# Top-8 from the gate columns, a TensorE transpose ahead of the down projection, and the down projection three half blocks earlier, in a fused state-space and routed-MLP kernel

## The chip, the cores and the metric

One core of a Trainium2 chip runs the whole kernel. The metric is the device time of one execution in microseconds (us), as the median of several runs. The profile is one further execution; its span is the time from its first to its last instruction.

## The reference

All large tensors are bf16. L is 2048 tokens, D is 1024 channels, P is 1024 states, and F is 3584.

```python
g = sigmoid((x * gate_w).sum(-1))                 # one gate for each token
# branch a: a diagonal complex state space layer
Bu = x @ B_bar.T                                  # complex, 1024 states
h_t = Lam_bar * h_{t-1} + Bu_t                    # scan over 2048 tokens
a = 2 * Re(hseq @ C.T) + x * Dskip
# branch b: an MLP on the 8 tokens with the largest score
r = x @ w_r ; idx = argsort(-r)[:8]
y = (silu(x[idx] @ w_gate) * (x[idx] @ w_up)) @ w_down * sigmoid(r[idx])
b = x ; b[idx] += y
out = g * a + (1 - g) * b
```

## The kernel before

**Stages.** The tokens are cut into 8 chunks k of 256. S1 multiplies x with the B matrices for a pair of chunks at a time (`s1`, PE line 266; `s1x`, line 282, for the first ones). ScalarE (ACT) copies the result from PSUM to V. VectorE (DVE) rotates it, scans it and rotates it back (`dve_m`, `dve_scan`, `dve_post`) into H[k]. S2 multiplies H[k] with the C matrices (`s2`, PE line 768): a chunk has two row blocks b of 128 tokens, and each row block has two halves dh of 512 channels, with 16 matmuls for a half. ACT then scales the half by the gate into ot (line 773). From block 2 on, ACT first presets the PSUM tile with x*D (`preset`, line 742, `KX = 1`); blocks 0 and 1 get x*(g*D + 1-g) by another way (`scale_x`, `mul_e`). The term (1-g)*x is written to the output by a DMA (`skip_x`), and `fin(b)` adds ot to it by an accumulating DMA on POOL's queue (line 794). The last two blocks add on DVE and are written by SyncE's queue (SP).

**The order.** It is written out by hand. PE, DVE, ACT and SP take their work exactly in program order. A list `blocks` gives the main loop, and its index n is the stage: n = 0 is S1 of chunks 2 and 3, n = 1 and 2 are S2 of chunks 0 and 1, n = 3 is S1 of chunks 4 and 5, n = 4 and 5 are S2 of chunks 2 and 3, n = 6 is S1 of chunks 6 and 7, and n = 7, 8, 9, 10 are S2 of chunks 4 to 7. `at((n, t), fn)` puts a piece of work into stage n: within an S2 stage, t below 1 means after the first half, t below 2 after the second, and so on.

**The router.** `gate_rows` (PE line 486) computes the scores r and the gate logits as rows: four groups of 512 tokens on partitions 0, 32, 64, 96. `gate_cols` turns them by four 128x128 TensorE transposes (zt, line 493) into columns, one column for each 128 tokens, and makes gcol and omgcol. The top 8 are found in two steps. `sel_a` copies the score rows (128 x 512) and `sel_a2` takes 8 candidates out of each row with DVE's max and index operations. `sel_b` gathers the 4 x 8 candidates of the four rows with one matmul (fl_ps, line 536), `sel_b2` takes the final 8 of 32 and starts the gather of their x rows (xsel). `sel_c` transposes xsel (xselT_ps, line 573).

**The MLP.** Its weights come in slots over SP's queue (`load_w`: wgu for gate and up, wd and wdb for down). `moe_slot` runs them on PE between the S2 and S1 stages: gate and up into pgu (line 660), later the down projection into y4 (the profile's y, line 672) as 112 matmuls that use 32 columns of the array each. Between the two, `silu_a` and `silu_b` make the gated activations gr1, and `silu_t` turns them into aT with a DMA transpose on SP's queue:

```python
def silu_t():
    nc.sync.dma_start_transpose(M["aT"][:].rearrange("p c j s -> p c (j s)"), M["gr", 1][:])
```

The last act is `sel_d` (the gate of the 8 tokens, zs_ps, line 589), `fin_a` (ACT copies y out as yc), `sel_c2`, `sel_d2` and `fin_b` (four small DVE operations on yc), `scatter_upd` (an accumulating indirect DMA on POOL's queue, line 752, then a read of the update ul for the last chunk on SP's), and `add_upd` on DVE for the last two blocks. The places of these in the list:

```python
at((7, 0.97), silu_t)
at((9, 2.88), sel_d)
at((9, 2.92), fin_a)
at((9, 2.95), lambda: (sel_c2(), sel_d2(), fin_b(), scatter_upd()))
pos = ... [(7, 0.9)] * 2 + [(9, 2.9)] * 7      # the 7 slots of the down projection
```

PSUM tiles of the router and the MLP share two buffers (pool `ps_m`, tag m), in turn; S2's tiles have two of their own.

Of the kernel before, what the change touches and what calls it, by code (L numbers as in the profile page):

```python
# [9 lines left out]
ALU = mybir.AluOpType  # L10
F32 = mybir.dt.float32
BF16 = mybir.dt.bfloat16
I32 = mybir.dt.int32
U32 = mybir.dt.uint32
PSUM = bass.MemoryType.PSUM

P = 128
LC = 256
# [6 lines left out]
def kernel(  # L25
# [19 lines left out]
    nc = tc.nc  # L45
# [6 lines left out]
    NTT = L // P  # L52
# [3 lines left out]
    NSEL = 8  # L56
# [9 lines left out]
    small = ctx.enter_context(tc.tile_pool(name="small", bufs=1))  # L66
    ps_s1 = ctx.enter_context(tc.tile_pool(name="ps_s1", bufs=2, space=PSUM))
    ps_s2 = ctx.enter_context(tc.tile_pool(name="ps_s2", bufs=2, space=PSUM))
    ps_m = ctx.enter_context(tc.tile_pool(name="ps_m", bufs=2, space=PSUM))
# [60 lines left out]
    ident = const.tile([P, P], BF16, name="ident")  # L130
    from concourse.masks import make_identity
    make_identity(nc, ident[:])
    ramp = const.tile([P, LC], F32, name="ramp")
    nc.gpsimd.iota(ramp[:], pattern=[[1, LC]], base=0, channel_multiplier=0, allow_small_or_imprecise_dtypes=True)
    jrow8 = small.tile([8, 4, 8], F32, name="jrow8")
    nc.gpsimd.iota(jrow8[:], pattern=[[2 * LC, 4], [0, 8]], base=LC, channel_multiplier=0, allow_small_or_imprecise_dtypes=True)
    M = {}
    rg = small.tile([P, KD, 32], BF16, name="rg")
    nc.gpsimd.memset(rg[:], 0.0)
    ones8 = small.tile([P, 8], BF16, name="ones8")  # L140
    nc.gpsimd.memset(ones8[:], 1.0)
    for i, v in enumerate((B_w_r, gate_w)):
        nc.gpsimd.dma_start(vrow[:, 3 + i, :], v.rearrange("(c p) -> c p", p=P))

# [329 lines left out]
    def sigm(pool, z_ap, shape, tagp):  # L474
        e = pool.tile(shape, BF16, name=tagp + "_e", tag={"sl": "mg"}.get(tagp, tagp))
        nc.scalar.activation(out=e[:], in_=z_ap, func=ACT.Sigmoid)
        return e

    gcol = small.tile([P, NTT], F32, name="gcol")
    omgcol = small.tile([P, NTT], F32, name="omgcol")  # L480

# [8 lines left out]
    def gate_cols():  # L490
        zt = ps_m.tile([P, 4, P], BF16, name="zt", tag="m")
        for tq in range(4):
            nc.tensor.transpose(zt[:, tq, :], M["zrb"][:, tq * P:(tq + 1) * P], ident[:])  # L493
        zv = zt[:].rearrange("p t (j s) -> p j t s", s=32)
        zb = small.tile([P, NTT], BF16, name="zb")
        nc.scalar.copy(out=zb[:].rearrange("p (j t) -> p j t", t=4), in_=zv[:, :, :, 1])
        gb = sigm(small, zb[:], [P, NTT], "gc")
        nc.scalar.copy(out=gcol[:], in_=gb[:])
        ob = small.tile([P, NTT], BF16, name="ob")
        nc.scalar.activation(out=ob[:], in_=gb[:], func=ACT.Copy, scale=-1.0, bias=1.0)  # L500
        nc.scalar.copy(out=omgcol[:], in_=ob[:])
        M["aT"] = small.tile([P, NFC // 4, 4, 32], BF16, name="aT", tag="va")

    nc.scalar.dma_start(Dbc[:], A_Dskip.rearrange("(o d) -> o d", o=1).to_broadcast([P, D]))
    M["xsel32"] = small.tile([P, KD, 32], BF16, name="xsel32", tag="wt")
# [2 lines left out]
    rowp = ctx.enter_context(tc.tile_pool(name="rowp", bufs=1))  # L508
# [3 lines left out]
    AX = mybir.AxisListType.X  # L512

    def sel_a():
        rT = rowp.tile([P, 2 * LC], F32, name="rT", tag="row8")
        nc.scalar.copy(out=rT[:], in_=M["zrb"][:])
        M["rT"] = rT

    def sel_a2():
        rT = M["rT"]  # L520
        mA = rowp.tile([P, NSEL], F32, name="mA")
        iA = rowp.tile([P, NSEL], U32, name="iA")
        nc.vector.max(out=mA[:], in_=rT[:])
        nc.vector.max_index(out=iA[:], in_max=mA[:], in_values=rT[:])
        iAf = rowp.tile([P, NSEL], F32, name="iAf")
        nc.vector.tensor_scalar(out=iAf[:], in0=iA[:], scalar1=-float(LC), scalar2=None, op0=ALU.add)
        mm = rowp.tile([P, 2, 4, NSEL], BF16, name="mm", tag="mg")
        eyeb = ident[:, 0:P:32].unsqueeze(2).to_broadcast([P, 4, NSEL])
        nc.vector.tensor_tensor(out=mm[:, 0], in0=mA[:].unsqueeze(1).to_broadcast([P, 4, NSEL]), in1=eyeb, op=ALU.mult)
        nc.vector.tensor_tensor(out=mm[:, 1], in0=iAf[:].unsqueeze(1).to_broadcast([P, 4, NSEL]), in1=eyeb, op=ALU.mult)  # L530
        M["mm"] = mm

    def sel_b():
        mm = M["mm"]
        fl_ps = ps_m.tile([NSEL, 2, 4 * NSEL], F32, name="fl_ps", tag="m")
        nc.tensor.matmul(fl_ps[:].rearrange("p k n -> p (k n)"), lhsT=ones8[:], rhs=mm[:].rearrange("p k j s -> p (k j s)"), start=True, stop=True)
        fl = rowp.tile([NSEL, 2, 4 * NSEL], F32, name="fl", tag="gr0")
        nc.scalar.copy(out=fl[:], in_=fl_ps[:])
        M["fl"] = fl

    def sel_b2():
        fl = M["fl"]
        cv = fl[:, 0, :]
        ci = rowp.tile([NSEL, 4 * NSEL], F32, name="ci", tag="mg")
        nc.vector.tensor_tensor(out=ci[:], in0=fl[:, 1, :], in1=jrow8[:].rearrange("p j s -> p (j s)"), op=ALU.add)
        gm = rowp.tile([NSEL, NSEL], F32, name="gm")
        kx = rowp.tile([NSEL, NSEL], U32, name="kx")
        nc.vector.max(out=gm[:], in_=cv)
        nc.vector.max_index(out=kx[:], in_max=gm[:], in_values=cv)
        kxf = rowp.tile([NSEL, NSEL], F32, name="kxf")  # L550
        nc.vector.tensor_copy(kxf[:], kx[:])
        dtmp = rowp.tile([NSEL, 2, NSEL], F32, name="dtmp")
        nc.vector.tensor_tensor(out=dtmp[:, 0, :], in0=kxf[:], in1=ident[:NSEL, :NSEL], op=ALU.mult)
        nc.vector.tensor_tensor(out=dtmp[:, 1, :], in0=gm[:], in1=ident[:NSEL, :NSEL], op=ALU.mult)
        dsel = rowp.tile([NSEL, 2], F32, name="dsel")
        nc.vector.reduce_sum(out=dsel[:], in_=dtmp[:], axis=AX)
        eq = rowp.tile([NSEL, 4 * NSEL], F32, name="eq", tag="gr1")
        nc.vector.tensor_scalar(out=eq[:], in0=ramp[:NSEL, 0:4 * NSEL], scalar1=dsel[:, 0:1], scalar2=None, op0=ALU.is_equal)
        nc.vector.tensor_tensor(out=eq[:], in0=eq[:], in1=ci[:], op=ALU.mult)
        tokf = rowp.tile([NSEL, 1], F32, name="tokf")  # L560
        nc.vector.reduce_sum(out=tokf[:], in_=eq[:], axis=AX)
        idx_c = small.tile([NSEL, 1], I32, name="idx_c")
        nc.vector.tensor_copy(idx_c[:], tokf[:])
        M["idx_c"] = idx_c
        xsel = rowp.tile([NSEL, D], BF16, name="xsel", tag="row8")
        nc.gpsimd.indirect_dma_start(out=xsel[:], out_offset=None, in_=x2d, in_offset=bass.IndirectOffsetOnAxis(ap=idx_c[:, :1], axis=0))
        M["xsel"] = xsel
        M["dsel"] = dsel
# [10 lines left out]
    def sel_c2():  # L579
        rs_b = M["rs_e"]  # L580
        rsel_c = small.tile([NSEL, 1], F32, name="rsel_c")
        nc.vector.tensor_copy(rsel_c[:], rs_b[:])
        M["rsel_c"] = rsel_c
# [10 lines left out]
    def sel_d2():  # L594
        gs_b = M["gs_e"]
        omg_b = rowp.tile([NSEL, 1], BF16, name="omg_b")
        nc.vector.tensor_scalar(out=omg_b[:], in0=gs_b[:], scalar1=-1.0, scalar2=1.0, op0=ALU.mult, op1=ALU.add)
        omg32 = small.tile([NSEL, 1], F32, name="omg32")
        nc.vector.tensor_copy(omg32[:], omg_b[:])
        M["omg32"] = omg32  # L600

    NG = 4
# [3 lines left out]
    NFB = FG // P  # L606
# [73 lines left out]
        nc.vector.tensor_tensor(out=up[:], in0=sl[:], in1=up[:], op=ALU.mult)  # L680

    def silu_t():
        nc.sync.dma_start_transpose(M["aT"][:].rearrange("p c j s -> p c (j s)"), M["gr", 1][:])

    def fin_a():
        yc = rowp.tile([NSEL, D], BF16, name="yc", tag="row8")
# [4 lines left out]
    def fin_b():  # L691
        yb = M["yc"]
        nc.vector.tensor_scalar(out=yb[:], in0=yb[:], scalar1=M["rsel_c"][:, 0:1], scalar2=M["omg32"][:, 0:1], op0=ALU.mult, op1=ALU.mult)
        M["upd"] = yb
# [56 lines left out]
    def scatter_upd():  # L751
        nc.gpsimd.indirect_dma_start(out=out2d[:, :], out_offset=bass.IndirectOffsetOnAxis(ap=M["idx_c"][:, :1], axis=0), in_=M["upd"][:], in_offset=None, bounds_check=L - 1, oob_is_err=False, compute_op=ALU.add)
        M["ul"] = const.tile([P, BPC, D], BF16, name="ul", tag=free_w.pop(0))
        nc.sync.dma_start(M["ul"][:], out2d[TLAST:, :].rearrange("(r p) d -> p r d", p=P))
# [48 lines left out]
    def at(pos, fn):  # L803
        pending.append((pos, len(pending), fn))
# [24 lines left out]
    at((2, 2.2), lambda: (scale_x(1), mul_e(1), load_x(5)))  # L829
    at((2, 3.5), lambda: (fin(0), fin(1)))  # L830
    at((3, 3.9), sel_c)
    at((9, 2.88), sel_d)
    at((3, 1.2), lambda: dve_m(3, 0, 8))
    at((3, 2.3), lambda: (skip_d(2), dve_scan(3, 0, 8)))
    at((3, 6.5), lambda: (skip_d(3), dve_post(3, 0, 8)))
# [21 lines left out]
    at((7, 0.96), silu_b)  # L857
    at((7, 1.2), lambda: (dve_scan0(6, 4, 8), dve_state(6, 0, 8)))
    at((7, 2.5), lambda: fin(8))
    at((7, 0.97), silu_t)  # L860
    at((7, 3.95), lambda: fin(9))
    at((7, 3.5), lambda: dve_post(6, 0, 8))
    at((7, 3.4), lambda: skip_d(6))
# [4 lines left out]
    at((9, 1.2), lambda: skip_x(14))  # L868
    at((9, 2.2), lambda: skip_x(15))
    at((8, 2.5), lambda: fin(10))  # L870
    at((9, 2.92), fin_a)
    at((8, 3.95), lambda: fin(11))
    at((9, 0.0), lambda: (skip_d(7), last_post(0, 0, NCT)))
    at((9, 0.1), lambda: last_m(1))
    at((9, 0.95), lambda: last_scan(1))
    at((9, 2.95), lambda: (sel_c2(), sel_d2(), fin_b(), scatter_upd()))
    at((9, 2.5), lambda: fin(12))
    at((9, 3.95), lambda: fin(13))
    at((9, 3.0), lambda: (last_post(1, 0, NCT // 2), last_post(1, NCT // 2, NCT)))
    at((10, 0.5), lambda: (add_upd(NTT - 2), add_upd(NTT - 1)))  # L880

    pos = [(3, 4.9)] * 2 + [(4, 1.9)] * 3 + [(5, 1.9)] * 3 + [(6, 1.9)] * 3 + [(6, 5.9)] * 3 + [(7, 0.9)] * 2 + [(9, 2.9)] * 7
    for s in range(NW // 2):
        at(pos[s], lambda s=s: moe_slot(s))

# [8 lines left out]
    for n, (m, k) in enumerate(blocks):  # L894
        free_w.extend(fill.get(n, ()))
        if n == 7:
            for pl in range(2):
                t = const.tile([P, 4, 2, D], BF16, name="wdb", tag=f"BT{pl}")
# [48 lines left out]
```

## Time and profile before

| | |
|---|---|
| median of 3 runs | 248.1 us (247.72 to 248.26) |
| profiled execution | 248.1 us, span 246.3 us |
| granted TensorE clock | 1.0 over the whole span |
| busy share | PE 98%, DVE 92%, ACT 48%, POOL 11% |
| instructions | 3573, of them PE 1405 matmuls and as many weight loads |
| DMA | 48.48 MB, 197 GB/s mean |

The 1.8 us between span and time lie outside the first and the last instruction. PE and DVE are both almost always busy, so the shares alone do not say which of them sets the time; the chain of waits does. A busy PE in these rows is a matmul's modelled start to end, and matmuls overlap, so costs on PE are read from the distance between groups and not from the busy time of one instruction.

### The profile page before, as it was taken

To read this page: it belongs to the slowest core of one execution; us is meant where nothing else is said; L and a number is where in the kernel's file an instruction comes from. 1 tells how busy PE (TensorE), PEld (TensorE's weight loads), DVE (VectorE), ACT (ScalarE), POOL (GpSimd) and SP (SyncE) were. 2 spreads that over 40 slices of the span, in tenths; PEclk is the share of its full clock that TensorE was granted. 3 is DMA by queue.
4 is the path that set the end of the run, shared out by engine and by line. 5 is a ranking of instruction groups with operands and counts; after the bars stand their busy time and mean duration, and the time that the engine had idled before them with its cause. 6 is when DMAs were issued, how large, how long until landed. Compare 5 with 4: busy or idle time off the path is not lost.

```text
span 246.3 us, 3573 instructions
## 1 busy us (share of the span) xinstructions
PE 240.7 (98%) x1405; PEld 115.3 (47%) x1405; DVE 225.8 (92%) x229; ACT 119.3 (48%) x203; POOL 26.9 (11%) x47
## 2 busy tenths in 40 slices
PE   8899999999999999999999999999999999999994
PEld 6664444444444444444444444444444444446453
DVE  1899999999999999999999999999999999999932
ACT  3699973233462572223355462235266445456411
POOL 4000000000000301520002040100000211110210
PEclk9999999999999999999999999999999999999999
DMA  7999999999760440766257989776699999962062
GB/s 187 224 135 244 226 229 217 276 215 257 253 191 0 118 140 0 150 108 213 88 190 229 352 230 320 239 285 249 184 359 284 385 304 302 111 128 35 3 146 69
DMA packets 65249, 48.48 MB, mean 197 GB/s; under 512 B 50496, under 2 KB 52160, under 8 KB 65232
## 3 DMA queue, kind: packets, MB, share of 16 engines
q1 hardware_dynamic: 60048, 37.46, 58.9%
q0 software_dynamic: 3264, 7.38, 14.5%
q10 hardware_dynamic: 1920, 3.41, 4.1%
q8 instruction: 11, 0.18, 0.3%
q14 instruction: 6, 0.05, 0.1%
HBM read 27.55 MB, written 8.40 MB: 146 GB/s over the span
## 4 chain that ended last, share of the span: by engine, by line
PE 95%; DMA 2%; SPq 1%; DVE 0%; issue 0%
PE vps L266 42%; PE zps L768 42%; PE zps L784 3%; PE pgu L660 3%; PE vps L282 2%; DMA BT<-in_A_B_im_dram 2%; PE y L672 1%; SPq L80 1%; PE zr L486 1%; SPq L77 0%; DVE ot L789 0%; PE xselT_ps L573 0%; PE zs_ps L589 0%; PE zt L493 0%; PE vb_ps L437 0%
## 5 line engine op out<-in xcount | busy, mean ns | idle before, releaser
L768 PE MATMUL zps<-CT,H 128*128 128x512 bf16 x480 | 105.0, 379 | 0.0
L266 PE MATMUL vps<-X,BT 128*128 128x512 bf16 x480 | 105.0, 379 | 0.0
L266 PEld LDWEIGHTS <-BT 128*128 128x128 bf16 x480 | 46.6, 98 | 56.8 <-PE pgu L660 0.7
L768 PEld LDWEIGHTS <-H 128*128 128x128 bf16 x480 | 46.5, 98 | 56.6 <-issue 1.3
L313 DVE TENSOR_TENSOR_SCAN U<-d,U 128x2048 bf16<-128x2048 f32 (+2 forms) x22 | 62.0, 2859 | 1.0 <-DVE U L304 0.5
L273 ACT CAST V<-vps 128x512 bf16<-128x512 f32 x60 | 32.2, 588 | 58.9 <-PE vps L266 58.8
L773 ACT ACTIVATE ot<-zps,gcol 128x512 bf16<-128x512 f32 x30 | 20.6, 686 | 46.3 <-PE zps L768 46.3
L742 ACT CAST zps<-xd 128x512 f32<-128x512 bf16 (+1 forms) x29 | 16.6, 576 | 3.6 <-ACT xt L729 3.3
L302 DVE TENSOR_TENSOR U<-V,T2tab 128x4096 bf16<-128x4096 bf16 (+2 forms) x11 | 16.6, 1511 | 0.6
L303 DVE TENSOR_TENSOR V<-V,nTi 128x4096 bf16<-128x4096 bf16 (+2 forms) x11 | 16.7, 1516 | 0.5
L304 DVE TENSOR_TENSOR U<-U,V 128x4096 bf16<-128x4096 bf16 (+2 forms) x11 | 16.7, 1516 | 0.4
L794 POOL DMA_DIRECT2D out_dram<-ot x14 | 13.0, 928 | 30.3 <-ACT ot L773 30.3
L338 DVE TENSOR_TENSOR U<-U,S2tab 128x4096 bf16<-128x4096 bf16 x7 | 16.0, 2292 | 0.2
L340 DVE TENSOR_TENSOR H<-H,U 128x4096 bf16<-128x4096 bf16 x7 | 16.0, 2292 | 0.2
L706 POOL DMA_DIRECT2D xt<-in_A_x_dram x12 | 7.2, 596 | 83.5 <-DMA out_dram<-xt 41.4
L729 ACT ACTIVATE xt<-xt,omgcol 128x1024 bf16<-128x1024 bf16 x14 | 16.0, 1144 | 0.0
L336 DVE TENSOR_TENSOR H<-U,Ctab 128x4096 bf16<-128x4096 bf16 x7 | 16.0, 2283 | 0.0
L371 DVE TENSOR_TENSOR_SCAN U<-D,U 128x1024 bf16<-128x1024 f32 x4 | 8.9, 2278 | 0.1
L724 DVE TENSOR_TENSOR xd<-xt,Dbc 128x1024 bf16<-128x1024 bf16 x14 | 9.0, 683 | 0.0
L282 PE MATMUL vps<-X,BT 128*128 128x256 bf16 x64 | 7.5, 273 | 1.2 <-DMA BT<-in_A_B_re_dram 0.6
L660 PE MATMUL pgu<-wgu,xsel 128*32 128x448 bf16 x128 | 7.2, 354 | 0.0
L282 PEld LDWEIGHTS <-BT 128*128 128x128 bf16 x64 | 6.0, 98 | 2.4 <-DMA BT<-in_A_B_re_dram 0.9
(155 smaller groups left out, 138.8 us busy)
## 6 DMA issues: line engine op xcount, KB each, us to landing
wgu<-in_B_w_gate_dram SPq DMA_DIRECT2D x16, 448.0 KB, 5.6
wgu<-in_B_w_up_dram SPq DMA_DIRECT2D x16, 448.0 KB, 6.6
out_dram<-ot POOLq DMA_DIRECT2D x14, 256.0 KB, 5.4
wdb<-in_B_w_down_dram SPq DMA_DIRECT2D x7, 512.0 KB, 10.5
xt<-in_A_x_dram POOLq DMA_DIRECT2D x12, 256.0 KB, 3.5
out_dram<-xt ACTq DMA_DIRECT2D x12, 256.0 KB, 5.4
wd<-in_B_w_down_dram SPq DMA_DIRECT2D x5, 512.0 KB, 10.3
xt<-in_A_x_dram SPq DMA_DIRECT2D x4, 256.0 KB, 4.2
```

The lines of the kernel that those rows point to most:

```text
L266: nc.tensor.matmul(o, lhsT=BT[pl][:, dc, ct * P:(ct + 1) * P], rhs=X[m][:, dc, k0 * LC:k1 * LC], start=(dc == 0), stop=(dc == KD - 1))
L273: nc.scalar.copy(out=V[k][:, :, ct, :], in_=vp[m, ct][:, :, kk, :])
L282: nc.tensor.matmul(vps[:, pl, c, :], lhsT=BT[pl][:, dc, ct * P:(ct + 1) * P], rhs=X[0][:, dc, k * LC:(k + 1) * LC], start=(dc == 0), stop= ...
L302: nc.vector.tensor_tensor(out=u, in0=v, in1=T2tab[:, :, c0:c1, :], op=ALU.mult)
L303: nc.vector.tensor_tensor(out=v, in0=v, in1=bc(nTi, c0, c1), op=ALU.mult)
L304: nc.vector.tensor_tensor(out=u, in0=u, in1=V[k][:, ::-1, c0:c1, :], op=ALU.add)
L313: nc.vector.tensor_tensor_scan(out=fl, data0=d0[:, c0:c1, :].rearrange("p c t -> p (c t)"), data1=fl, initial=0.0, op0=ALU.mult, op1=ALU.add)
L336: nc.vector.tensor_tensor(out=h, in0=g, in1=bc(Ctab, c0, c1), op=ALU.mult)
L338: nc.vector.tensor_tensor(out=g, in0=g, in1=S2tab[:, :, c0:c1, :], op=ALU.mult)
L742: nc.scalar.copy(out=z[:], in_=xd[b][:, d_:d_ + w])
L768: nc.tensor.matmul(zps[:], lhsT=H[k][:, pl, ct, tl * P:(tl + 1) * P], rhs=CT[pl][:, ct, dsl], start=(fresh and ct == 0 and pl == 0), stop= ...
L773: nc.scalar.activation(out=ots[b][:, dsl], in_=zps[:], func=ACT.Copy, scale=gcol[:, b:b + 1])
```

## The change

The note that comes with the change says that row blocks 2 and 3 also have x*D preset in PSUM, and that their (1-g)*x and the fp32 product of block 0 moved into S2 of chunks 0 and 1. The diff has no edit of `preset`, `KX`, `scale_x`, `skip_x` or of their places in the list: they are the same in both kernels. What the diff holds is this.

- The first step of the top 8 works on 16 rows of 128 tokens in place of 4 rows of 512. `gate_cols` keeps the score columns (rcb), `sel_a` transposes them on PE to 16 x 128 (rT_ps), and the candidates become 16 x 8 = 128. `sel_b` has two matmuls of 128 columns in place of one of 64, and the tiles of `sel_b2` are 8 x 128 wide in place of 8 x 32.
- `silu_t` transposes gr1 with seven 128x128 TensorE transposes and one ACT copy, in place of the DMA transpose. It stands after the first half of stage 8 (chunk 5) in place of the first half of stage 7 (chunk 4). aT is cleared once by POOL.
- `sel_d`, the seven slots of the down projection and `fin_a` stand after the last half of stage 8 in place of the third half of stage 9: three halves earlier. `sel_c2`, `sel_d2`, `fin_b` and `scatter_upd` stand after the first half of stage 9, ahead of `last_scan(1)` on DVE.

```diff
-    jrow8 = small.tile([8, 4, 8], F32, name="jrow8")
+    jrow8 = small.tile([8, NTT, 8], F32, name="jrow8")
...
+    rcb = small.tile([P, NTT], BF16, name="rcb")
...
         nc.scalar.copy(out=gcol[:], in_=gb[:])
+        nc.scalar.copy(out=rcb[:].rearrange("p (j t) -> p j t", t=4), in_=zv[:, :, :, 0])
...
         M["aT"] = small.tile([P, NFC // 4, 4, 32], BF16, name="aT", tag="va")
+        nc.gpsimd.memset(M["aT"][:], 0.0)
...
     def sel_a():
-        rT = rowp.tile([P, 2 * LC], F32, name="rT", tag="row8")
-        nc.scalar.copy(out=rT[:], in_=M["zrb"][:])
+        rT_ps = ps_m.tile([NTT, P], BF16, name="rT_ps", tag="m")
+        nc.tensor.transpose(rT_ps[:], rcb[:], ident[:])
+        rT = rowp.tile([NTT, P], F32, name="rT", tag="row8")
+        nc.scalar.copy(out=rT[:], in_=rT_ps[:])
...
-        mA = rowp.tile([P, NSEL], F32, name="mA")
+        mA = rowp.tile([NTT, NSEL], F32, name="mA")
         nc.vector.max(out=mA[:], in_=rT[:])
         nc.vector.max_index(out=iA[:], in_max=mA[:], in_values=rT[:])
-        nc.vector.tensor_scalar(out=iAf[:], in0=iA[:], scalar1=-float(LC), scalar2=None, op0=ALU.add)
+        nc.vector.tensor_copy(iAf[:], iA[:])
...
-        fl_ps = ps_m.tile([NSEL, 2, 4 * NSEL], F32, name="fl_ps", tag="m")
-        nc.tensor.matmul(fl_ps[:].rearrange("p k n -> p (k n)"), lhsT=ones8[:], rhs=mm[:].rearrange("p k j s -> p (k j s)"), start=True, stop=True)
+        fl_ps = ps_m.tile([NSEL, 2, NTT * NSEL], F32, name="fl_ps", tag="m")
+        for k in range(2):
+            nc.tensor.matmul(fl_ps[:, k, :], lhsT=ones16[:], rhs=mm[:, k].rearrange("k j s -> k (j s)"), start=True, stop=True)
...
     def silu_t():
-        nc.sync.dma_start_transpose(M["aT"][:].rearrange("p c j s -> p c (j s)"), M["gr", 1][:])
+        aT_ps = ps_m.tile([P, NFB, NG, 32], BF16, name="aT_ps", tag="m")
+        for c in range(NFB):
+            nc.tensor.transpose(aT_ps[:, c].rearrange("p j s -> p (j s)"), M["gr", 1][:, c * P:(c + 1) * P], ident[:])
+        nc.scalar.copy(out=M["aT"][:, :, :, 0:NSEL], in_=aT_ps[:, :, :, 0:NSEL])
...
-    at((9, 2.88), sel_d)
+    at((8, 3.88), sel_d)
...
-    at((7, 0.97), silu_t)
+    at((8, 0.8), silu_t)
...
-    at((9, 2.92), fin_a)
+    at((8, 3.92), fin_a)
...
-    at((9, 2.95), lambda: (sel_c2(), sel_d2(), fin_b(), scatter_upd()))
+    at((9, 0.15), lambda: (sel_c2(), sel_d2(), fin_b(), scatter_upd()))
...
-    pos = ... + [(7, 0.9)] * 2 + [(9, 2.9)] * 7
+    pos = ... + [(7, 0.9)] * 2 + [(8, 3.9)] * 7
```

More of the change, by code (lines that the diff above doesn't have):

```diff
@@ L134 @@
     nc.gpsimd.iota(ramp[:], pattern=[[1, LC]], base=0, channel_multiplier=0, allow_small_or_imprecise_dtypes=True)
-    jrow8 = small.tile([8, 4, 8], F32, name="jrow8")
-    nc.gpsimd.iota(jrow8[:], pattern=[[2 * LC, 4], [0, 8]], base=LC, channel_multiplier=0, allow_small_or_imprecise_dtypes=True)
+    jrow8 = small.tile([8, NTT, 8], F32, name="jrow8")
+    nc.gpsimd.iota(jrow8[:], pattern=[[P, NTT], [0, 8]], base=0, channel_multiplier=0, allow_small_or_imprecise_dtypes=True)
     M = {}
@@ L139 @@
     nc.gpsimd.memset(rg[:], 0.0)
-    ones8 = small.tile([P, 8], BF16, name="ones8")
-    nc.gpsimd.memset(ones8[:], 1.0)
+    ones16 = small.tile([NTT, 8], BF16, name="ones16")
+    nc.gpsimd.memset(ones16[:], 1.0)
     for i, v in enumerate((B_w_r, gate_w)):
@@ L520, in sel_a2 @@
         rT = M["rT"]
-        mA = rowp.tile([P, NSEL], F32, name="mA")
-        iA = rowp.tile([P, NSEL], U32, name="iA")
+        mA = rowp.tile([NTT, NSEL], F32, name="mA")
+        iA = rowp.tile([NTT, NSEL], U32, name="iA")
         nc.vector.max(out=mA[:], in_=rT[:])
         nc.vector.max_index(out=iA[:], in_max=mA[:], in_values=rT[:])
-        iAf = rowp.tile([P, NSEL], F32, name="iAf")
-        nc.vector.tensor_scalar(out=iAf[:], in0=iA[:], scalar1=-float(LC), scalar2=None, op0=ALU.add)
[L527 to L530, printed above, removed]
+        iAf = rowp.tile([NTT, NSEL], F32, name="iAf")
+        nc.vector.tensor_copy(iAf[:], iA[:])
+        mm = rowp.tile([NTT, 2, NTT, NSEL], BF16, name="mm", tag="mg")
+        eyeb = ident[:NTT, :NTT].unsqueeze(2).to_broadcast([NTT, NTT, NSEL])
+        nc.vector.tensor_tensor(out=mm[:, 0], in0=mA[:].unsqueeze(1).to_broadcast([NTT, NTT, NSEL]), in1=eyeb, op=ALU.mult)
+        nc.vector.tensor_tensor(out=mm[:, 1], in0=iAf[:].unsqueeze(1).to_broadcast([NTT, NTT, NSEL]), in1=eyeb, op=ALU.mult)
         M["mm"] = mm
@@ L534, in sel_b @@
         mm = M["mm"]
-        fl_ps = ps_m.tile([NSEL, 2, 4 * NSEL], F32, name="fl_ps", tag="m")
-        nc.tensor.matmul(fl_ps[:].rearrange("p k n -> p (k n)"), lhsT=ones8[:], rhs=mm[:].rearrange("p k j s -> p (k j s)"), start=True, stop=True)
-        fl = rowp.tile([NSEL, 2, 4 * NSEL], F32, name="fl", tag="gr0")
+        fl_ps = ps_m.tile([NSEL, 2, NTT * NSEL], F32, name="fl_ps", tag="m")
+        for k in range(2):
+            nc.tensor.matmul(fl_ps[:, k, :], lhsT=ones16[:], rhs=mm[:, k].rearrange("k j s -> k (j s)"), start=True, stop=True)
+        fl = rowp.tile([NSEL, 2, NTT * NSEL], F32, name="fl", tag="gr0")
         nc.scalar.copy(out=fl[:], in_=fl_ps[:])
@@ L543, in sel_b2 @@
         cv = fl[:, 0, :]
-        ci = rowp.tile([NSEL, 4 * NSEL], F32, name="ci", tag="mg")
+        ci = rowp.tile([NSEL, NTT * NSEL], F32, name="ci", tag="mg")
         nc.vector.tensor_tensor(out=ci[:], in0=fl[:, 1, :], in1=jrow8[:].rearrange("p j s -> p (j s)"), op=ALU.add)
@@ L556, in sel_b2 @@
         nc.vector.reduce_sum(out=dsel[:], in_=dtmp[:], axis=AX)
-        eq = rowp.tile([NSEL, 4 * NSEL], F32, name="eq", tag="gr1")
-        nc.vector.tensor_scalar(out=eq[:], in0=ramp[:NSEL, 0:4 * NSEL], scalar1=dsel[:, 0:1], scalar2=None, op0=ALU.is_equal)
+        eq = rowp.tile([NSEL, NTT * NSEL], F32, name="eq", tag="gr1")
+        nc.vector.tensor_scalar(out=eq[:], in0=ramp[:NSEL, 0:NTT * NSEL], scalar1=dsel[:, 0:1], scalar2=None, op0=ALU.is_equal)
         nc.vector.tensor_tensor(out=eq[:], in0=eq[:], in1=ci[:], op=ALU.mult)
@@ L880 @@
     at((10, 0.5), lambda: (add_upd(NTT - 2), add_upd(NTT - 1)))
-    pos = [(3, 4.9)] * 2 + [(4, 1.9)] * 3 + [(5, 1.9)] * 3 + [(6, 1.9)] * 3 + [(6, 5.9)] * 3 + [(7, 0.9)] * 2 + [(9, 2.9)] * 7
+    pos = [(3, 4.9)] * 2 + [(4, 1.9)] * 3 + [(5, 1.9)] * 3 + [(6, 1.9)] * 3 + [(6, 5.9)] * 3 + [(7, 0.9)] * 2 + [(8, 3.9)] * 7
     for s in range(NW // 2):
```

## The prediction, made before the changed kernel ran

> **What bounds the kernel now.** I read the page first: PE is busy 98% of the span and DVE 92%. The chain of waits, by engine and line, then says which of the two counts.
>
> ```profile
> PE 240.7 (98%) x1405; PEld 115.3 (47%) x1405; DVE 225.8 (92%) x229; ACT 119.3 (48%) x203; POOL 26.9 (11%) x47
> ...
> PE 95%; DMA 2%; SPq 1%; DVE 0%; issue 0%
> ```
>
> The chain is 95% PE, and DVE's share is nil. Next I asked for PE's own waits. These are all of them:
>
> ```profile
> PE wps L149 <- DVE halfpi L129: 1.1, 1, 1.1
> PE vps L282 <- DMA BT<-in_A_B_re_dram: 0.6, 1, 0.6
> PE vps L282 <- DMA BT<-in_A_B_im_dram: 0.6, 1, 0.6
> ```
>
> They belong to the start, which the change doesn't touch. From there to the last matmul at 242.98 us PE waits for nobody. So any array time that is added to PE adds to the total, and time saved on DVE, ACT, POOL or the DMA queues returns nothing until one of them makes PE wait. Third, the same chain in order of time prices a group of small matmuls (start, length, what):
>
> ```profile
> 61.93 3.56 PE vps L266 x16
> 65.49 0.22 PE zt L493 x4
> 65.71 17.27 PE zps L768 x80
> 82.98 0.12 PE fl_ps L536
> 83.10 10.46 PE zps L768 x48
> 93.57 13.81 PE vps L266 x64
> 107.38 0.28 PE xselT_ps L573 x8
> 107.67 3.56 PE vps L266 x16
> ```
>
> A full matmul takes 17.27/80 = 0.2159 us, so one column takes 0.2159/512 = 0.42 ns. The four 128x128 transposes zt cost 0.22, or 0.055 each, and what follows them runs at its usual pace. fl_ps has 64 columns, which would be 0.03, but takes 0.12, and the 48 matmuls after it take 10.46 where 48 x 0.2159 = 10.36: it costs 0.22 in all. The same 0.1 follows xselT_ps (3.56 for 16 where 16 x 0.2159 = 3.45). So a full-size transpose slips in for its columns alone, and a matmul that uses only 8 columns or 8 rows of the array costs about 0.2 more than its columns, half before and half after.
>
> **The change on PE, part by part.**
>
> The seven transposes of gr1 are full-size, like zt: 7 x 0.055 = 0.39. Nothing hides them, since PE has no gap. Lower bound: xselT_ps's 0.28/8 = 0.035 each, 0.25 in all. Upper bound: zt's mean duration in the groups by line, 0.219, if nothing overlaps, 7 x 0.219 = 1.53. I take 0.39, because zt has the same shape and stands beside the same line 768.
>
> The Trainium skill, page "TensorE: Matmul & The Clock Gate", section "Part 4: PE-mode transpose", speaks against the change: it gives about 275 ns for a 128x128 bf16 transpose inside a kernel and says the fast clock doesn't engage for it. By that page the seven and rT_ps would take 8 x 0.275 = 2.2 us and the time would be 250.3 or so; the zt row has 0.055 at a granted clock of 1.0, and I go by the row.
>
> rT_ps is a new transpose with 16 columns of weights and 128 streamed columns, after the first half of chunk 0. Its nearest row is fl_ps (8 columns of weights): 0.22 plus 64 more columns x 0.42 ns = 0.25. Lower bound: a zt transpose, 0.055. Upper bound: xselT_ps's whole group, 0.28 + 0.11 = 0.39. I take 0.25.
>
> fl_ps becomes two matmuls of 128 columns: 256 - 64 = 192 more columns, 0.08. Lower bound 0 (hidden in the pause that the row shows); upper bound another 0.22, if the second pays the pause again. I take 0.08.
>
> The down projection and zs_ps are moved and not changed: the same 112 and 8 matmuls in the same order, between two halves of line 768 as before. 0, with +-0.1 for the pauses at their edges.
>
> Sum on PE: 0.39 + 0.25 + 0.08 = 0.72 us. The profiled execution took 248.1, the same as the median of the runs, so 248.1 + 0.72 = 248.8.
>
> **Edits that I cost at nothing, and their cover.**
>
> Waits that PE could gain: the transposes need gr1, which DVE finishes at 193.97, and PE reaches them near 201.7.
>
> ```profile
> 193.35 0.62 DVE L680 TENSOR_TENSOR gr<-sl_e,gr 128x896 bf16<-128x896 bf16 x1
> ...
> 201.52 0.69 ACT L773 ACTIVATE ot<-zps,gcol 128x512 bf16<-128x512 f32 x1 [2.15 <-PE zps L768]
> 202.10 1.04 ACT L350 COPY D<-d 128x1024 f32<-128x1024 f32 x1
> ...
> 203.04 0.59 ACT L742 CAST zps<-xd 128x512 f32<-128x512 bf16 x1
> ```
>
> The new ACT copy of aT (128 x 224 from PSUM: between zs_b's 0.14 and the 128x512 cast's 0.59; I take 0.35) stands between L350 and the preset L742 of this timeline. That preset ends at 203.63, and PE needs it one half after 201.4, at 204.8; PE is now 0.39 later itself, so some 1.2 us of cover stay. Without them the half would start 0.35 late.
>
> The down weights are needed earlier. zs_ps began at 222.20; three halves (3 x 3.45) earlier is 211.85, and PE's added 0.72 makes 212.6, so the first y is due near 212.8. In the timeline the last wd group starts 2.63 after the first (224.89 after 222.26), so it is due near 215.4. The tile view of wd gives for the last transfer, issued at 197.2:
>
> ```profile
> L639 SPq DMA_DIRECT2D wd<-in_B_w_down_dram x1: 368/368/368, 197.2 to 197.2; - x1
> ...
> DMA to landing us min/median/max: 15.8/15.8/15.8
> ```
>
> It lands at 213.0, with 2.4 us to spare, and the last wdb (195.1 + 13.4 = 208.5) is further ahead of its use. SP's queue before them is the same. The DMA transpose that is removed (SPq L683, 8.58 us from 198.61) stood behind them and only competed for the engines, so they should land earlier. It also stood on SP alone: the next SP item is the read of ul at 233.4, so nothing moves up with it.
>
> ACT waits for y near 212.9 to 215.9 and then makes yc (1.49) before the next preset, exactly as at 225.61, where the preset ended at 227.58 and PE needed it at 228.95: 1.4 us of cover again.
>
> DVE: fin_b and its three small operations (0.12 + 0.13 + 0.14 + 0.53) now stand ahead of the scan that began at 224.57. yc is ready near 217.5, so DVE doesn't wait. They already stood ahead of the last rotation, so H[7] comes when it did (first part 232.0, second 234.06), and PE needs it at 236.02. Behind the waiting fin_b is only that scan. The candidates: MAX8 0.69 and FIND_INDEX8 0.68 shrink towards the 0.18 and 0.17 of the 8x32 rows (-1.0); (0.69 - 0.18)/480 gives 1.06 ns for a column, so six operations on 96 more columns add 0.6. DVE gains 0.4 and ends no wait of PE.
>
> ACT: rT 0.61 becomes about 0.2, rcb adds 0.20, fl goes from 0.20 to at most yc's 0.36; this falls near 68.4 and 85. The first ot of line 773 ended at 70.92 and PE needs its buffer at 65.71 + 2 x 3.45 = 72.6, and the preset after fl ended at 85.87 and is needed at 83.10 + 3.45 = 86.55: 1.7 and 0.7 us of cover. POOL: clearing aT costs 896/256 x 0.31 = 1.1 us near 66, and POOL idles until 80.0. The scatter now goes ahead of fin(12) on POOL's queue, so fin(12) moves from 219.76 to some 229, behind the scatter; its buffer isn't used again before the end. The read of ul lands near 233 in place of 237.2, and DVE's wait of 3.28 goes:
>
> ```profile
> DVE xt L757 <- DMA ul<-out_dram: 3.3, 1, 3.3
> ```
>
> What is late next is ot of block 14 at 236.74, and behind that the last matmul, so the end doesn't move.
>
> The presets that the announcement speaks of are the same in both kernels: 0.
>
> **The rivals.** About 0.2% (0.5 us) is what a measurement of this kernel can tell from no change, so slower begins at 248.6.
>
> First rival, not slower: the pause isn't paid at rT_ps, because its 16 columns with 128 rows run like a zt transpose, and fl_ps's extra columns fall into its own pause. Place: 69 us and 83 us. Then PE gains 0.39 + 0.055 = 0.44, and the time is 248.5. It decides if the two router groups together add less than 0.11. For it: the pause is seen only at 8 columns, 8 rows and 32-column groups. Against it: zr, with 32 columns in four groups, also shows 3.56 after it.
>
> Second rival, faster: PE's pace improves where the DMA transpose loaded the engines (DMA share 1.27 from 200 to 210 us). Against it: the 160 matmuls from 187.56 took 34.64, 0.2165 each, 0.0006 above 0.2159; all of it returned is 0.1 us, which doesn't cancel 0.72. The end beyond the last matmul is 3.3 us with DMAs that land in 1.7 to 1.8, so 0.1 there. I see 248.6 at best from both, and faster only by something unseen.
>
> Third rival, much slower: the down weights arrive late. It decides once the last wd lands after 215.4; each us beyond that is a us. If its 15.8 us grew by a quarter (4 us), 1.6 us would be lost: 250.4. Against it is the lighter queue. Transposes that don't overlap would give 0.72 + 1.14 = 1.86, 250.0, as well.
>
> **How the numbers follow.** Forecast (PE grows by 0.6 to 0.9): 0.68. First rival: 0.17. Second: 0.05. Late weights, a late preset or transposes that don't overlap: 0.10. The range reaches from 248.4 (the lower bounds 0.25 + 0.055 + 0) to 249.4, which takes in the upper bounds of the two router groups (0.39 + 0.39 + 0.22 = 1.0) and 0.3 of a short new wait, and leaves out the third rival. Faster by over 0.2%: 0.05. Within 0.2%: the first rival and some spread of the forecast's low side, 0.20. Slower: 0.75.
>
> **What would show it.** In the changed chain: a piece aT_ps x7 of 0.39 near 201.5, rT_ps of about 0.15 near 69 with 0.1 in the piece after it, fl_ps near 0.2, y at 212.8, and the last matmul's end near 243.7. PE's waits should still be only those of the start. A wait of PE on wd, xd or aT, or an aT_ps piece of over 1 us, would show the forecast wrong; a wait of DVE on yc would show the cover of the scan misread.

## The result, and the profile after

The changed kernel takes 248.9 us (median of 5 runs, 248.72 to 249.51) against 248.07 for the kernel before: a ratio of 1.004, 95% interval 1.0024 to 1.0056. It is slower by about 0.8 us. The forecast was 248.8. The profiled execution has a span of 247.1 us at a granted clock of 1.0. All ratios here are of the runs within 1.5% of their kernel's shortest, which leaves out five of the eight runs of e3 and one of the six of e8 (656.78 us).

The page's shares and the head of the chain, and then all waits of PE, read as before:

```profile
PE 242.0 (98%) x1414; PEld 116.0 (47%) x1414; DVE 225.6 (91%) x229; ACT 119.2 (48%) x205; POOL 31.7 (13%) x48
...
PE 95%; DMA 2%; SPq 1%; DVE 0%; issue 0%
```

```profile
PE wps L149 <- DVE halfpi L129: 1.1, 1, 1.1
PE vps L282 <- DMA BT<-in_A_B_im_dram: 0.5, 1, 0.5
PE va_ps L161 <- DMA vrow<-in_A_Lambda_im_dram: 0.2, 1, 0.2
```

PE still waits for nobody after the start, and PE is still 95% of the chain. The changed places in the chain in order of time (start, length, what):

```profile
65.52 0.22 PE zt L494 x4
65.74 3.45 PE zps L777 x16
69.19 0.15 PE rT_ps L519
69.34 13.92 PE zps L777 x64
83.27 0.20 PE fl_ps L542 x2
83.47 10.47 PE zps L777 x48
...
201.84 0.39 PE aT_ps L691 x7
202.23 10.36 PE zps L777 x48
212.59 0.22 PE zs_ps L595 x6
...
215.94 20.83 PE zps L777 x96
236.77 6.96 PE zps L793 x48
243.73 0.02 issue
```

rT_ps takes 0.15, and the 64 matmuls behind it 13.92 where 64 x 0.2159 is 13.82: 0.25 in all. fl_ps takes 0.20 in place of 0.12, with the same 0.1 behind it. aT_ps takes 0.39 and what follows runs at its usual pace.

The start of a run varies by itself (the first unit of line 266 begins at 15.00 us before, at 15.22 after, and at 16.36 in one of the experiments below; in the first two the chain follows it back to the landing of a load of BT, at 9.30 and 9.52). So I compare kernels by the distance from zt's start to the last matmul's end: 242.98 - 65.49 = 177.49 before, 243.73 - 65.52 = 178.21 after. The difference is 0.72.

### The profile page after: what moved, and what is told of

Same layout as the page of the kernel before. It is cut to its first block, busy times and chain, and to the rows that moved or that the text cites. A ratio compares the mean times of both kernels' runs of the same rounds, so it can differ in the third digit from the quotient of the medians.

```text
span 247.1 us, 3595 instructions
## 1 busy us (share of the span) xinstructions
PE 242.0 (98%) x1414; PEld 116.0 (47%) x1414; DVE 225.6 (91%) x229; ACT 119.2 (48%) x205; POOL 31.7 (13%) x48
## 4 chain that ended last, share of the span: by engine, by line
PE 95%; DMA 2%; SPq 1%; DVE 0%; issue 0%
PE zps L777 42%; PE vps L266 42%; PE zps L793 3%; PE pgu L666 3%; PE vps L282 2%; DMA BT<-in_A_B_im_dram 2%; PE y L678 1%; SPq L80 1%; PE zr L487 1%; SPq L77 0%; DVE ot L798 0%; PE aT_ps L691 0%; PE xselT_ps L579 0%; PE zs_ps L595 0%; PE zt L494 0%
## 5 line engine op out<-in xcount | busy, mean ns | idle before, releaser
L266 PEld LDWEIGHTS <-BT 128*128 128x128 bf16 x480 | 46.5, 98 | 56.8 <-issue 0.8
L793 PE MATMUL zps<-CT,H 128*128 128x256 bf16 (+1 forms) x48 | 7.1, 308 | 0.0
```

The costliest lines, as they stand in the source:

```text
L266: nc.tensor.matmul(o, lhsT=BT[pl][:, dc, ct * P:(ct + 1) * P], rhs=X[m][:, dc, k0 * LC:k1 * LC], start=(dc == 0), stop=(dc == KD - 1))
```

## The experiments

Theory: PE is the only bound, and the change adds 0.72 us to PE, of which the columns are one part and pauses at changes of the used array shape the other.

| kernel | zt to end | against before | ratio to before, 95% interval |
|---|---|---|---|
| before | 177.49 | | |
| changed | 178.21 | +0.72 | 1.004 (1.0024 to 1.0056) |
| e1, TensorE transpose alone | 177.88 | +0.39 | 1.001 (0.9994 to 1.0025) |
| e2, router part alone | 177.83 | +0.34 | 1.0013 (0.9995 to 1.003) |
| e4, changed, rT_ps full-size | 178.01 | +0.52 | 1.0016 (0.9997 to 1.0035) |
| e5, before, fl_ps full-size | 177.29 | -0.20 | 0.9987 (0.9967 to 1.0007) |
| e7, 8 small transposes together | 178.14 | +0.65 | 1.0023 (1.0003 to 1.0044) |
| e8, 8 small transposes apart | 179.57 | +2.08 | 1.0076 (1.0046 to 1.0106) |
| e9, 8 full transposes apart | 177.94 | +0.45 | 1.0016 (0.9996 to 1.0035) |

The timed intervals of e1, e2, e4, e5 and e9 include a ratio of 1, so their times alone don't tell them from the kernel before. The distances in the chain are what tells these kernels apart, and every interval holds the ratio that its distance gives. Each distance is from one profile; e6 below, which changes nothing on PE, gives the changed kernel's 178.21 again.

### The parts of the change, one at a time

e1 has the TensorE transposes of gr1 alone (with the ACT copy and POOL's clearing of aT that belong to them):

```diff
-        nc.sync.dma_start_transpose(M["aT"]..., M["gr", 1][:])
+        for c in range(NFB):
+            nc.tensor.transpose(aT_ps[:, c]..., M["gr", 1][:, c * P:(c + 1) * P], ident[:])
+        nc.scalar.copy(out=M["aT"][:, :, :, 0:NSEL], in_=aT_ps[:, :, :, 0:NSEL])
...
-    at((7, 0.97), silu_t)
+    at((8, 0.8), silu_t)
```

> The kernel before, with one part of the change alone: gr1 is transposed by seven TensorE transposes and an ACT copy after the first half of chunk 5, and the rest stays as it was, the down projection in its old place too. Theory (PE is the only bound and a full-size transpose costs its 128 columns): a piece of 0.39 us in the chain, nothing after it, the last matmul's end 0.39 later, the time 248.5 (+0.4). Rival (the cost of the change lies in the router or in the end of the kernel, and transposes fit in beside other work): 248.1. Rival (transposes don't overlap, 0.219 each): +1.5, 249.6.

The time was 248.34 us beside 247.93 for the kernel before in the same session. The chain of e1:

```profile
201.28 0.39 PE aT_ps L686 x7
201.67 20.72 PE zps L772 x96
```

0.39, and 20.72/96 = 0.2158 behind it: no pause. The theory holds.

e2 has the router part alone (rcb, rT_ps, two fl_ps matmuls, wide sel_b2), with the DMA transpose and the late down projection kept.

> The kernel before, with the other PE part alone: the top 8 from the 16 gate columns (rT_ps, two fl_ps matmuls, wider sel_b2); the DMA transpose and the late down projection stay. Theory (array shape changes cost 0.2 beside the columns): rT_ps 0.15 with 0.1 behind it, fl_ps 0.20 in place of 0.12, together +0.33, the time 248.4. Rival (only the columns count): +0.05 + 0.08 = 0.13, 248.2. Rival (the smaller DVE work gives something back): at or below 248.1.

248.43 beside 247.93, and +0.34 in the chain; the column-only rival (0.13) falls, and so does the gain by DVE. The two places in the chain of e2:

```profile
69.11 0.15 PE rT_ps L518
69.26 13.92 PE zps L773 x64
83.18 0.20 PE fl_ps L541 x2
83.38 10.47 PE zps L773 x48
```

0.39 + 0.34 = 0.73 adds up to the whole change's 0.72.

e3 has the moved places alone, with the DMA transpose kept:

```diff
-    at((9, 2.88), sel_d)
+    at((8, 3.88), sel_d)
...
-    at((9, 2.92), fin_a)
+    at((8, 3.92), fin_a)
...
-    at((9, 2.95), lambda: (sel_c2(), sel_d2(), fin_b(), scatter_upd()))
+    at((9, 0.15), lambda: (sel_c2(), sel_d2(), fin_b(), scatter_upd()))
...
-    pos = ... + [(9, 2.9)] * 7
+    pos = ... + [(8, 3.9)] * 7
```

> The kernel before, with the places of sel_d, the down projection, fin_a and of the scatter group moved as in the change, but with the DMA transpose of gr1 kept. Theory: the DMA transpose stands on the same queue behind the last down weights, which land at 213.0 in the profile before, so aT lands at 213 to 217 and PE, which is due at 212, waits for it 1 to 5 us: 249 to 253, with a wait of PE on the DMA of aT in its waits. Rival (the transpose runs beside the queue's backlog, some 9 us after its issue at 198.6): it lands near 208, PE doesn't wait, and the move by itself costs nothing: 248.1.

The eight runs of this kernel scatter from 253.05 to 259.33, with a median of 257.28 beside 247.93 for the kernel before. The three shortest, up to 254.18, give the ratio 1.0209 (1.0167 to 1.0251). The profiled run, 259.09, is among the five longer ones: its profile shows where the time of such a run went, and none of a shorter one was taken. PE's longest wait, and the chain:

```profile
PE y L672 <- DMA aT<-gr: 7.7, 1, 7.7
```

```profile
202.37 18.10 DMA aT<-gr
220.52 5.64 PE y L672 x60
226.16 20.83 PE zps L768 x96
```

The transpose was issued at 202.37 and landed at 220.5, which is later than I expected, and the wait cost more than itself. The windows of e3 (PE, weight loads, DVE, ACT, POOL busy, then the granted clock, DMA share and GB/s) show the second part of the loss:

```profile
210.00:216.00 6.00, 2.80 (x20) 1.21 (x18) 5.86 (x4) 2.35 (x5) 0.85 (x1) 0.94 1.24 165
216.00:222.00 6.00, 1.48 (x32) 1.09 (x36) 5.90 (x8) 0.00 (x0) 0.00 (x0) 0.50 0.80 150
222.00:228.00 6.00, 6.00 (x97) 3.84 (x90) 3.36 (x8) 1.75 (x5) 0.00 (x0) 0.71 0.01 3
```

The granted clock fell to 0.50 during the wait, and the down projection ran 5.64 us in place of 3.11; its mean granted clock (220.5 to 226.1) was 0.56, and 3.11/0.56 is 5.55. From zt to the end this run took 187.77, which is 10.28 more than before: 7.7 for the wait, 2.5 for the slower projection. So the theory holds in kind and undersized the loss, and the rival (the move costs nothing with the DMA transpose) falls. In the changed kernel, with the transposes on PE, the same move costs nothing.

### The price of a small matmul between full ones

e4 pads the score columns to 128, so that rT_ps is a full-size transpose; e5 gives fl_ps of the kernel before 128 columns of ones:

```diff
# e4, against the changed kernel
-    rcb = small.tile([P, NTT], BF16, name="rcb")
+    rcb = small.tile([P, P], BF16, name="rcb")
+    nc.gpsimd.memset(rcb[:], 0.0)
...
-        rT_ps = ps_m.tile([NTT, P], BF16, name="rT_ps", tag="m")
+        rT_ps = ps_m.tile([P, P], BF16, name="rT_ps", tag="m")
# e5, against the kernel before
-    ones8 = small.tile([P, 8], BF16, name="ones8")
+    ones8 = small.tile([P, P], BF16, name="ones8")
...
-        fl_ps = ps_m.tile([NSEL, 2, 4 * NSEL], F32, name="fl_ps", tag="m")
+        fl_ps = ps_m.tile([P, 2, 4 * NSEL], F32, name="fl_ps", tag="m")
```

> The changed kernel, with the score columns padded with zeros from 16 to 128, so that rT_ps is a full-size 128x128 transpose of which only 16 rows are used. Theory (the 0.2 of rT_ps is a pause for the change of the array's used shape): the piece is 0.055 with nothing after it, 0.20 less than in the changed kernel, 248.7. Rival (any single inserted group pays the pause, by its wait on ACT or by being alone): 0.25 as before, 248.9.

> The kernel before, with fl_ps at full array size: 128 columns of ones as weights in place of 8, the result on 128 partitions of which 8 are read. Theory (shape pause): fl_ps costs its 64 columns, 0.03, in place of 0.22, so the last matmul ends 0.19 earlier and the time is 247.9, too little for the runs to tell but plain in the chain. Rival (single groups always pause): 0.22 as it was, 248.1.

The chain of e4 and then of e5, at the same two places as above:

```profile
68.89 0.06 PE rT_ps L520
68.95 13.81 PE zps L778 x64
```

```profile
84.14 0.03 PE fl_ps L536
84.17 10.36 PE zps L768 x48
```

More array work, less time: rT_ps went from 0.25 to 0.06, and fl_ps from 0.22 to 0.03, each 0.20 from zt to the end. e5 is by that 0.20 us ahead of the kernel before and 0.92 ahead of the changed one in the chain. Its time (248.23 beside 248.6 for the kernel before) doesn't establish a gain: the interval 0.9967 to 1.0007 includes none.

e7, e8 and e9 add eight transposes that nothing reads to the kernel before:

```diff
+    def dummy(n, w):
+        ...
+            nc.tensor.transpose(M["dum"][0:w, :], ident[:, 0:w], ident[:])
+    at((1, 1.95), lambda: dummy(8, 16))                  # e7
...
+    for p_ in [(1, 0.95), (1, 1.95), (1, 2.95), (1, 3.95), (2, 1.95), (2, 2.95), (2, 3.95), (3, 1.95)]:
+        at(p_, lambda: dummy(1, 16))                     # e8; dummy(1, P) in e9
```

> The kernel before with eight added transposes that nothing reads, 16 columns of weights and 128 streamed columns each like rT_ps, all together between two halves of chunk 0. Theory (one pause for each change of shape): 8 x 0.055 + 0.2 = 0.64, 248.7. Rival (a pause for each small matmul): 8 x 0.25 = 2.0, 250.1. Rival (no pause): 0.44, 248.5.

> The kernel before with the same eight transposes that nothing reads, one each at eight places between halves or units of full matmuls in stages 1, 2 and 3. Theory (a pause for each change of shape): 8 x 0.25 = 2.0, 250.1. Rival (no pause): 0.44, 248.5. A value between the two would say that the pause depends on what stands around it.

> The kernel before with eight added full-size 128x128 transposes that nothing reads, one each at the eight places of the run with eight small ones apart. Theory (a pause only where the used shape of the array changes): 8 x 0.055 = 0.44 from zt to the last matmul's end, 177.9 in place of 177.49, and a time of about 248.5. Rival (any group that stands alone pauses): 8 x 0.25 = 2.0, 179.5.

Chain of e7, then PE's timeline of e8, then the chain of e9:

```profile
72.38 0.54 PE dum L819 x8
72.92 10.47 PE zps L768 x48
```

```profile
69.80 0.22 PE L819 MATMUL dum<-ident 128*16 128x128 bf16 x1
69.95 3.63 PE L768 MATMUL zps<-CT,H 128*128 128x512 bf16 x16
73.51 0.22 PE L819 MATMUL dum<-ident 128*16 128x128 bf16 x1
73.67 3.63 PE L768 MATMUL zps<-CT,H 128*128 128x512 bf16 x16
77.22 0.22 PE L819 MATMUL dum<-ident 128*16 128x128 bf16 x1
```

```profile
70.20 0.06 PE dum L819
70.26 3.45 PE zps L768 x16
73.71 0.06 PE dum L819
```

Together, eight cost 0.54 + 0.11: 8 x 0.055 and one pause of 0.2. Apart, one transpose and a half of 16 matmuls take 73.51 - 69.80 = 3.71, where the 16 alone take 3.45: 0.26 each and 2.08 in all. Full-size ones take 0.06 each, also alone. So the pause belongs to the change of the used shape, not to the count, nor to standing alone, nor to the wait on ACT. The Trainium skill, page "TensorEngine Tiling (Array Packing)", section "Key Properties", says that a change of the tiling mode drains the engine. e8 against e9 shows a pause that would fit this, 0.2 us for the way to 16-column weights and back, a price that the page doesn't give; whether the pause is that drain, no run here shows.

### The scatter beside the scan

In the changed kernel the scatter's issue on POOL takes 5.29 us in place of 1.56. e6 puts the group behind the last scan; e10 leaves it early and adds four multiplications on DVE, over a V that is read no more, between it and the scan.

```diff
# e6, against the changed kernel
-    at((9, 0.15), lambda: (sel_c2(), sel_d2(), fin_b(), scatter_upd()))
+    at((9, 0.96), lambda: (sel_c2(), sel_d2(), fin_b(), scatter_upd()))
# e10, against the changed kernel
+    def stand_in():
+        v = V[NK - 1][:, :, :, P:2 * P]
+        for _ in range(4):
+            nc.vector.tensor_tensor(out=v, in0=v, in1=nTi[...]..., op=ALU.mult)
...
+    at((9, 0.16), stand_in)
```

> The changed kernel, with the scatter group (the three small operations, fin_b, the scatter and the read of ul) behind the last scan on DVE in place of ahead of it. In the changed kernel's profile the scatter's issue on POOL took 5.29 us beside that scan, and 1.56 in the kernel before. Theory (DVE's scan holds up POOL's indirect issue): the issue takes 1.5 to 2 us and starts near 230.7, so the update is read at about the same time. Rival (it waits for something else, as a DMA in flight from the output writes near 226): it takes 1.5 too, but only by the later start, which this run can't tell from the theory; if it takes 5 us again, the theory is wrong. In both the total stays that of the changed kernel, 248.9, since ul isn't on PE's path.

> The changed kernel with four added DVE multiplications (128x2048, bf16, written over a V that is read no more) between fin_b and the last scan, so that the scatter is issued at the same time, near 226, but beside multiplications and not beside the scan. Theory (the scan holds up the indirect issue on POOL): 1.6 us. Rival (the early start holds it up: something that is still in flight near 226): 5.3 us again. Second rival (any long DVE work holds it): about 4.9, the length of the four. H[7] comes some 5 us later, so PE may wait up to 1 us at the last block, and the time may be up to 250.

The scatter in the timeline of the changed kernel, then in that of e10, and then in that of e6:

```profile
225.77 4.45 DVE L371 TENSOR_TENSOR_SCAN U<-D,U 128x1024 bf16<-128x1024 f32 x2
226.16 5.29 POOL L761 DMA_INDIRECT out_dram<-yc,idx_c  x1 [11.70 <-DVE yc L702]
```

```profile
224.77 4.99 DVE L887 TENSOR_TENSOR V<-V,nTi 128x2048 bf16<-128x2048 bf16 x4
225.16 2.11 POOL L761 DMA_INDIRECT out_dram<-yc,idx_c  x1 [11.22 <-DVE yc L702]
```

```profile
230.68 1.57 POOL L761 DMA_INDIRECT out_dram<-yc,idx_c  x1 [16.01 <-DVE yc L702]
```

Beside the scan the issue ends 1.2 us after the scan does; beside the multiplications, at nearly the same time of the run, it takes 2.11. Behind the scan (e6) it takes 1.57. In e3, too, the issue took 5.28, at 228.59 beside a scan that began at 228.20. The early start isn't the cause, and neither is a transfer still in flight: the DMA share was 0.00 from 226.1 to 231.5 in the changed kernel. A busy DVE as such isn't the cause either. But one of the multiplications is shorter (1.2 us) than one of the scans (2.3 us). Whether that length counts, or something else in the scan, wasn't tried. Both kernels took the changed kernel's time within the noise (248.88 in e6, with a ratio to before of 1.0038; e10's one run, 248.68), and e6 has the same 178.21 from zt to the end: the update is off PE's path.

## Why the prediction was right, point by point

- **The bound.** PE waits for nothing after the start in both kernels, and the sum on PE, 0.72, is the 0.72 from zt to the end. The median moved by 0.83, with an interval of 0.6 to 1.4; the tenth beyond the sum is within the runs' spread.
- **The seven transposes.** Taken 0.39, measured 0.39 (e1 too). The non-overlapping bound of 1.53 falls. The 275 ns that the Trainium skill gives ("TensorE: Matmul & The Clock Gate", "Part 4: PE-mode transpose") isn't what a transpose adds here: the aT_ps row has seven in 0.39 at a granted clock of 1.0, though one of them, from its start to its modelled end, has 0.219.
- **rT_ps.** Taken 0.25 from the fl_ps row, measured 0.15 + 0.10; e4 shows that 0.2 of it is the pause. The first rival, that 16 columns with 128 rows don't pause, is refuted by this row and by e8.
- **fl_ps.** Taken +0.08, measured 0.20 against 0.12: +0.08.
- **The move.** Taken 0, and it costs 0 in the changed kernel. I hadn't said that it depends on the TensorE transpose: e3 shows that with the DMA transpose alone it costs 5 to 11 us.
- **The second rival.** In e1, without the DMA transpose, the same 160 matmuls take 13.92 + 20.72 = 34.64, as in the kernel before. So nothing was there to win. The 0.1 that I had put down to the DMA's load stands in the 64 matmuls behind pgu (13.92), and the same 13.92 follows pgu at 130.72, long before that DMA.
- **ACT's cover.** The aT copy took 0.35 (203.40), the preset behind it ended at 204.23 and PE needed it at 202.23 + 3.45 = 205.68: 1.4 us of cover where I had reckoned 1.2.

Three side steps failed or were too sure, and cost nothing here. First, I said the last down weights "should land earlier" without the DMA transpose. The tile view of wd in the changed kernel, and the start of the last wd group in PE's timeline:

```profile
L645 SPq DMA_DIRECT2D wd<-in_B_w_down_dram x1: 367/367/367, 197.4 to 197.4; - x1
...
DMA to landing us min/median/max: 17.0/17.0/17.0
```

```profile
215.28 0.66 PE L678 MATMUL y<-wd,aT 128*32 128x256 bf16 x16
```

They landed at 214.4, later than the 213.0 before, and the last wd group starts at 215.28: the cover was 0.9 us and not 2.4. One pair doesn't settle the sign, though. From issue to landing this transfer took 13.9 to 17.0 in the five profiles without the DMA transpose (changed, e1, e4, e6, e10) and 15.8 to 18.8 in the seven with it, so it tends to land earlier without it, but scatters by 3 us. The third rival was nearer than I had put it. Second, the read of ul was to land near 233 and landed at 236.9, because of the scatter's long issue (the read was issued at 232.98, and at 228.80 in e10, where the scatter's issue took 2.11): DVE waited 2.48 for it, where it had waited 3.28 before. Third, DVE's gain of 0.4 was 0.2 (225.8 to 225.6 busy): MAX8 and FIND_INDEX8 on 16 x 128 took 0.28 and 0.27, not 0.18 and 0.17.

## What to carry to other kernels

When the chain is PE almost from end to end and PE waits for nobody, price an edit by the time it adds on PE and then check, wait by wait, that nothing new reaches PE; work saved on other engines returns nothing. Small matmuls between full ones are cheaper when padded to the full array, or when put side by side, because the change of shape costs 0.2 us here and the padding costs PE nothing. Before moving a consumer forward, check where its producer's transfer lands: moved past a slow DMA it cost up to 11 us, while the same move with the transpose on PE was free.

## What the runs showed of the hardware that I had not expected

- The DMA transpose of gr1 (128 x 896, bf16) took 18.1 us from issue to landing in e3, while the last transfer of wd took 13.9 to 18.8 in the profiles here.
- In the profiled run of e3 a PE wait of 7.7 us cost a further 2.5: the granted clock fell to 0.50 in the wait, and the next 112 small matmuls ran at 0.56 on average (5.64 in place of 3.11).
- A weight change from full to 16 or 8 columns and back cost PE 0.2 us, and eight 16-column transposes side by side paid it once (0.65 in all, against 2.08 apart).
- An indirect DMA's issue on POOL took 5.29 us beside DVE's scan, 2.11 beside bf16 multiplications and 1.57 after the scan. A plain POOL issue beside another such scan took 0.85 (213.61, scan from 211.50 to 215.97), as elsewhere.
